# Batch 0 of a fused attention and two FFNs: both heads in one product, zeros beside keys and values, and two weight pieces made earlier

## Chip, cores and metric

One core of one Trainium2 chip. The metric is the device time of one execution in microseconds (us). The kernel before takes 851.62 us, the median of 3 runs (851.27 to 851.75).

## What is computed

Attention with a window mask (4 batches, 8 heads, 576 positions, head size 64), and then two FFNs over the 2304 tokens, all in float32:

```python
scores = scale * np.matmul(q, k.transpose(0, 1, 3, 2))
mask_plain = (rel >= 0) & (rel < 32)                          # heads 0 to 3
mask_dil = (rel >= 0) & (rel < 128) & (rel % 4 == 0)          # heads 4 to 7
attn = softmax(np.where(mask, scores, -1e9))                  # sum + 1e-9
x = (attn @ v) as (2304, 512)
h = x @ w_in                                                  # FFN 1, d_ff 2048
x = (np.maximum(h, 0) + alpha * np.minimum(h, 0)) @ w_out
h = x @ w_in2                                                 # FFN 2
out = np.where(h >= 1, h, np.where(h <= -1, 0, (h + 1) ** 2 / 4)) @ w_out2
```

## The kernel before

**Attention in groups.** The host reorders the positions of the dilated heads, so that each block of 32 queries needs 64 neighbouring keys. A batch then has 6 groups (NGB), and the 4 batches 24 (NG). A group holds 3 x 4 blocks (n, j) of 32 queries, for two heads at once; the upper 64 partitions hold the second head's data. Each group goes through the same steps: scores (TensorE, the mask is added by a product with the identity), maximum and subtraction (VectorE), exp (ScalarE), turn (TensorE transposes, ScalarE copies the result to pT), values (TensorE), norm (VectorE: sum, reciprocal, product) and out (TensorE transposes, ScalarE copies into XA, the input of FFN 1).

**Batch 0 has its own form** (`e_scores` L166, `e_exp` L184, `e_values` L195). One tile `e_in` per group, six in all, holds keys, queries and values; each group is loaded by two DMAs over all 128 partitions (L119, L127) from the array `a0`. The two heads are separate products of 64 rows, 12 blocks x 2 heads for scores (L180) and as many for values (L204); float32 products count twice in the profile, so 48 each. Scores and values have one PSUM tile each, of two banks (tags s2 and o2).

**Batches 1 to 3** use `a_scores` L133 and `a_values` L216: one product of 128 rows for both heads. For that, `qk` (two buffers) holds keys of head 0 with zeros beside them for head 1, and the reverse in the upper half; `vz` (two buffers) does so for the values. The loads L122, L123 and L131 fill 64 partitions each, the last in runs of 4 x 65 floats. The zeros are written once, by memsets on GpSimd (L745 to L749 and, for the whole of qk0, L803).

**Weights.** A weight piece (128 x 1024 words, 512 KB) is loaded by `w_load` L265 into one of five staging tiles and made into float32 by three VectorE steps (`w_make` L308: L320, L321, L314). `conv(k)` issues the next k such steps; `more()` loads further pieces while staging tiles are free. A made piece of w_in is split into a high and a low part by ScalarE (L326) and GpSimd or VectorE (L327), in `w_split`; the input XA is split the same way in `x_split` L423.

**The order is written out by hand** (`tc.manual_schedule()`): every engine, and the DMA queue of SyncE (SP), works through its instructions in program order. At the start SP issues the loads of all six groups of batch 0, with one weight piece behind group 0 and one behind group 2 (FIRST), and TensorE runs 10 warm-up products. The loop at L786 then runs the six groups, each a step behind the next (scores of group i, turn of i-1, out of i-2, values of i-1), and at i = 0 and 2 makes a weight piece. At i = 3, after the first x_split and the memset of qk0, SP gets the loads of group 6 (the first of batch 1) and the next pieces. Behind the loop (L810 to L833) stand the last steps of groups 4 and 5, four conv steps and the first hidden products of FFN 1 (`f_h` L503, for two f, in quarters by input chunk c; L513, L514 and L515 are its three products), each behind the x_split of its chunk.

Then come the slots (`slot` L898), one per f: hidden product f, activation, output product of the f before (`f_y`, L688 to L690), one attention step of a later batch, and conv steps. The constants EARLY (5, 6) say how many conv steps slots 0 and 1 issue; from slot 2 on it is 6.

Of the kernel before, what the change touches and what calls it, by code (L numbers as in the profile page):

```python
# [22 lines left out]
P = 128  # L23
# [35 lines left out]

EARLY = (5, 6)  # L60
READY = 12
# [20 lines left out]
def _key_offset(g, m):  # L82

    return SUB * m + (WIN if g % 3 == 1 and m >= 6 else 0)


@with_exitstack
def attention_then_two_ffns(ctx: ExitStack, tc: tile.TileContext, a0, aqk, av, w1i, w1o, w2i, w2o, alpha, masks, ident, out):
    nc = tc.nc
# [19 lines left out]
    vzt = [wp.tile([P, VZ], F32, tag=f"vz{i}", name=f"vz{i}") for i in range(2)]  # L109
    vz = [t[:, :GS * 2 * 4 * DS].rearrange("p (n h j d) -> p n h j d", n=GS, h=2, j=4) for t in vzt]  # L110

# [3 lines left out]


    def a_load_qk(i):
        if i < NGB:
            nc.sync.dma_start(e_in[i][:, :QK], a0[i, :, :QK])  # L119
        elif i < NG:  # L120
            t = qk[i % 2]
            nc.sync.dma_start(t[:D, :QK], aqk[i - NGB, :D])  # L122
            nc.sync.dma_start(t[D:, KW:], aqk[i - NGB, D:])  # L123

    def a_load_v(i):
        if i < NGB:
            nc.sync.dma_start(e_in[i][:, QK:], a0[i, :, QK:])  # L127
        elif i < NG:
            for h in range(2):
                r = slice(h * D, (h + 1) * D)  # L130
                nc.sync.dma_start(vz[i % 2][r, :, h].rearrange("p n j d -> p n (j d)"), av[i - NGB, r])  # L131

    def a_scores(i, pool, tag, add_on_pe):  # L133
        ps = pool.tile([P, GS, 2, KEYS], F32, tag=tag, name="s_ps")
        sb0 = (i % NGB) * GS
        t = qk[i % 2]
        mk = mask[:, sb0:sb0 + GS, None, :].to_broadcast([P, GS, 2, KEYS])
# [27 lines left out]

    def e_scores(i):  # L166

        ps = ps_e.tile([P, 2, TW], F32, tag="s2", name="s_ps")
        t = e_in[i]
        mk = mask[:, i * GS:(i + 1) * GS]  # L170
        for h in range(2):
            nc.tensor.matmul(ps[:, h, :GS * KEYS].rearrange("p (n k) -> p n k", n=GS), idb, mk, start=True, stop=False)
        for n in range(GS):
            for j in range(4):
                r = slice(j * SUB, (j + 1) * SUB)
                k0 = _key_offset(i, 4 * n + j)
                for h in range(2):
                    p = slice(h * D, (h + 1) * D)
                    q = t[p, KW + n * P + j * SUB:KW + n * P + (j + 1) * SUB]
                    nc.tensor.matmul(ps[r, h, n * KEYS:(n + 1) * KEYS], q, t[p, k0:k0 + KEYS], start=False, stop=n == GS - 1)  # L180
        sc_t[i] = ps

    def e_exp(i):
        ps = sc_t.pop(i)  # L184
        s = buf(i, "s").rearrange("p (n k) -> p n k", k=KEYS)
        src = ps[:, :, :GS * KEYS].rearrange("p h (n k) -> p h n k", n=GS)
        mx = st_p.tile([P, 2 * GS], F32, tag="mx", name="mx")
        mx = mx.rearrange("p (h n) -> p h n", h=2)
        nc.vector.tensor_reduce(mx, src, AX.X, ALU.max)
        nc.vector.tensor_tensor(  # L190
            s.rearrange("p (n h) k -> p h n k", h=2), src, mx[:, :, :, None].to_broadcast([P, 2, GS, KEYS]), ALU.subtract)
        nc.scalar.activation(s, s, AF.Exp, scale=SCALE)
        s_t[i] = s

    def e_values(i):  # L195
        pT = pT_t.pop(i)
        ps = ps_e.tile([P, 2, TW], F32, tag="o2", name="o_ps")
        v = e_in[i][:, QK:].rearrange("p (n j d) -> p n j d", n=GS, j=4)
        for n in range(GS):
            for j in range(4):  # L200
                r = slice(j * SUB, (j + 1) * SUB)
                for h in range(2):
                    p = slice(h * D, (h + 1) * D)
                    nc.tensor.matmul(ps[r, h, n * DS:(n + 1) * DS], pT[p, n, r], v[p, n, j], start=True, stop=True)  # L204
        a_norm(i, ps[:, :, :GS * DS].rearrange("p h (n d) -> p n h d", n=GS))

    def a_turn(i, pool, tag):
# [8 lines left out]
    def a_values(i, pool, tag):  # L216
        pT = pT_t.pop(i)
        ps = pool.tile([P, GS, 2, DS], F32, tag=tag, name="o_ps")
        for n in range(GS):
            for j in range(4):  # L220
                r = slice(j * SUB, (j + 1) * SUB)
                nc.tensor.matmul(ps[r, n], pT[:, n, r], vz[i % 2][:, n, :, j], start=True, stop=True)  # L222
        a_norm(i, ps)
# [488 lines left out]
    with tc.manual_schedule(), ExitStack() as late:  # L712
        first = ExitStack()
        sp = first.enter_context(tc.tile_pool(name="sp", bufs=1))
        ps_e = first.enter_context(tc.tile_pool(name="ps_e", bufs=1, space=bass.MemoryType.PSUM))
        e_in = [sp.tile([P, QK + GS * 4 * DS], F32, name=f"e_in{i}") for i in range(NGB)]

# [16 lines left out]

        for i in range(NGB):
            a_load_qk(i)
            a_load_v(i)
            if i in FIRST:
                w_load(*pend_l.pop(0))
            if i == 1:  # L740
                nc.sync.dma_start(mask[:, 2 * GS:], masks[:, 2 * GS:])
        nc.sync.dma_start(al, alpha)
        nc.scalar.activation(half, half, AF.Exp, scale=0.0)
        nc.scalar.activation(half, half, AF.Copy, scale=0.5)
        nc.gpsimd.memset(qk[1][:D, QK:], 0.0)  # L745
        nc.gpsimd.memset(qk[1][D:, :KW], 0.0)
        for i in range(2):
            nc.gpsimd.memset(vz[i][:D, :, 1], 0.0)
            nc.gpsimd.memset(vz[i][D:, :, 0], 0.0)  # L749

# [13 lines left out]
        def more():  # L764

            while not hold and pend_l and st_free:
                w_load(*pend_l.pop(0))
# [18 lines left out]
        for i in range(NGB):  # L786
            e_scores(i)
            if i >= 1:
                a_turn(i - 1, ps_a, "a")
            e_exp(i)  # L790
            if i >= 2:
                a_out(i - 2, ps_a, "w")
            else:
                fill(2)
            if i >= 1:
                e_values(i - 1)
            w_cut()
            if i in FIRST:
                conv(3)
            if i == 3:  # L800
                x_split(n0, 0, True)

                nc.gpsimd.memset(qk[0], 0.0)  # L803
                hold = False
                a_load_qk(NGB)
                w_load(*pend_l.pop(0))
                w_load(*pend_l.pop(0))
                a_load_v(NGB)
                more()
            if i == 4:  # L810
                x_split(n0, 1, True)
        w_cut()
# [4 lines left out]
        conv(1)  # L817
        e_values(NGB - 1)
        x_split(n0, 2)
# [314 lines left out]
def _attention_layout(q, k, v):  # L1134
# [67 lines left out]
```

## Time and profile before

| What | us |
|---|---|
| median of 3 runs | 851.62 |
| lowest and highest run | 851.27 and 851.75 |
| the profiled execution | 853.01 |
| its span, first to last instruction | 851.2 |
| TensorE busy in the span | 835.7 |
| VectorE busy | 556.0 |
| GpSimd busy | 483.4 |
| ScalarE busy | 428.6 |

The profile is of one execution. PE is TensorE, PEld its weight loads (which lie beside its products), DVE is VectorE, ACT ScalarE, POOL GpSimd, SP SyncE, which issues the DMAs. A name such as L514 is a line of the kernel. Times in views are counted from the first instruction. "DMA share" is the mean busy share of the core's 16 DMA engines, and "PEclk" the clock that TensorE was granted, as a share of 2.4 GHz.

### The profile page before, as it was taken

What the parts mean: (1) busy time and instruction counts of PE and PEld (TensorE: products, weight loads), DVE (VectorE), ACT (ScalarE), POOL (GpSimd) and SP (SyncE); (2) the same over time, 40 slices, a digit from 0 to 9 for tenths busy, and PEclk for the clock granted to TensorE, in tenths of its full rate; (3) what the DMA queues carried; (4) which work ended last, traced back from release to release, by engine and by line L of the source; (5) the groups of instructions that cost most, each with busy time, mean ns of one, the idle gap of its engine ahead of it and who ended that gap; (6) DMA issues with size and microseconds to landing.
All of it is one profiled execution on the core that took longest, in us unless ns stands there. A gap on an engine that the chain in (4) does not pass through costs nothing.

```text
span 851.2 us, 14291 instructions
## 1 busy us (share of the span) xinstructions
PE 835.7 (98%) x5330; PEld 687.2 (81%) x5330; DVE 556.0 (65%) x911; ACT 428.6 (50%) x803; POOL 483.4 (57%) x411
## 2 busy tenths in 40 slices
PE   6999999999999999999999999999999999999998
PEld 3667778998777878888888888888888888888898
DVE  4798787666775676766688776776428677640243
ACT  3444444665435565555444565564435555443364
POOL 2465656777434677667348666763652423346486
PEclk9899999999999999999999999999999999999999
DMA  8798665864630025354287745243836553547210
GB/s 301 226 259 233 200 170 178 262 192 132 199 118 25 1 83 202 112 163 159 99 334 292 264 157 209 105 181 123 314 128 218 192 181 126 171 152 293 77 74 25
DMA packets 54980, 147.45 MB, mean 173 GB/s; under 512 B 5632, under 2 KB 13440, under 8 KB 54912
## 3 DMA queue, kind: packets, MB, share of 16 engines
q1 hardware_dynamic: 54624, 146.39, 51.1%
q8 instruction: 42, 0.69, 0.3%
q14 instruction: 26, 0.21, 0.1%
q10 hardware_dynamic: 288, 0.16, 0.1%
HBM read 101.97 MB, written 44.56 MB: 172 GB/s over the span
## 4 chain that ended last, share of the span: by engine, by line
PE 81%; DVE 7%; DMA 5%; ACT 3%; issue 2%; POOL 1%; SPq 0%; ACTq 0%; DVEq 0%; POOLq 0%
PE y L688 14%; PE y L690 14%; PE y L689 14%; PE h_ps L544 7%; PE h_ps L545 7%; PE h_ps L546 7%; PE h_ps L513 5%; PE h_ps L515 4%; PE h_ps L514 4%; DMA gd<-XA 3%; PE o_ps L222 2%; PE s_ps L148 1%; ACT wr L326 1%; PE t_ps L211 1%; DVE w_ps L320 1%
## 5 line engine op out<-in xcount | busy, mean ns | idle before, releaser
L327 POOL TENSOR_TENSOR wol<-wo,woh 128x512 fp32r<-128x512 f32 x153 | 201.2, 1322 | 76.6 <-ACT woh L326 76.2
L688 PE MATMUL y<-gh,wol 128*128 128x512 f32 (+1 forms) x444 | 164.0, 369 | 0.6 <-POOL wol L327 0.6
L690 PE MATMUL y<-gl,woh 128*128 128x512 f32 (+1 forms) x444 | 160.2, 361 | 0.0
L689 PE MATMUL y<-gh,woh 128*128 128x512 f32 (+1 forms) x444 | 160.1, 361 | 0.0
L327 POOL TENSOR_TENSOR wr<-wb,wr 128x512 fp32r<-128x512 f32 x60 | 77.8, 1297 | 124.6 <-ACT wr L326 123.7
L327 POOL TENSOR_TENSOR wr<-wi,wr 128x512 fp32r<-128x512 f32 x50 | 64.6, 1293 | 124.3 <-ACT wr L326 123.0
L544 PE MATMUL h_ps<-xv,wr 128*128 128x512 f32 x336 | 130.8, 389 | 0.2 <-DVE wf L314 0.2
L545 PE MATMUL h_ps<-xv,wr 128*128 128x512 f32 x336 | 130.8, 389 | 0.0
L546 PE MATMUL h_ps<-xv,wr 128*128 128x512 f32 x336 | 130.8, 389 | 0.0
L326 ACT ACTIVATE woh<-wo 128x512 fp32r<-128x512 f32 x153 | 93.6, 626 | 67.6 <-PE y L690 51.0
L688 PEld LDWEIGHTS y<-gh,wol 128*128 128x128 f32 x444 | 83.7, 189 | 16.6 <-POOL wol L327 2.3
L690 PEld LDWEIGHTS y<-gl,woh 128*128 128x128 f32 x444 | 83.6, 188 | 13.3
L689 PEld LDWEIGHTS y<-gh,woh 128*128 128x128 f32 x444 | 83.8, 189 | 12.2
L513 PE MATMUL h_ps<-xv,wr 128*128 128x512 f32 (+1 forms) x256 | 90.2, 352 | 0.4
L514 PE MATMUL h_ps<-xv,wr 128*128 128x512 f32 (+1 forms) x256 | 86.2, 337 | 0.2 <-DVE xv L327 0.2
L515 PE MATMUL h_ps<-xv,wr 128*128 128x512 f32 (+1 forms) x256 | 86.4, 337 | 0.0
L558 ACT ACTIVATE g<-g,half 128x512 f32<-128x512 f32 x64 | 44.8, 723 | 72.2 <-DVE g L557 71.0
L689 PE MATMUL y<-gx,woh 128*128 128x512 f32 x192 | 75.4, 392 | 0.0
L690 PE MATMUL y<-gx,woh 128*128 128x512 f32 x192 | 75.3, 392 | 0.0
L688 PE MATMUL y<-gx,wol 128*128 128x512 f32 x192 | 75.3, 392 | 0.0
L544 PEld LDWEIGHTS h_ps<-xv,wr 128*128 128x128 f32 x336 | 63.1, 188 | 13.8 <-issue 0.6
L545 PEld LDWEIGHTS h_ps<-xv,wr 128*128 128x128 f32 x336 | 63.1, 188 | 13.2
(122 smaller groups left out, 1515.1 us busy)
## 6 DMA issues: line engine op xcount, KB each, us to landing
gd<-XA SPq DMA_DIRECT2D x42, 512.0 KB, 3.4
gx<-gd SPq DMA_DIRECT2D x42, 512.0 KB, 6.5
wb<-whole SPq DMA_DIRECT2D x30, 512.0 KB, 4.6
st<-w1i SPq DMA_DIRECT2D x16, 512.0 KB, 6.0
st<-w1o SPq DMA_DIRECT2D x16, 512.0 KB, 6.0
st<-w2i SPq DMA_DIRECT2D x16, 512.0 KB, 4.6
st<-w2o SPq DMA_DIRECT2D x16, 512.0 KB, 4.7
kept<-wr SPq DMA_DIRECT2D x16, 512.0 KB, 2.7
```

What stands on the lines that cost most here:

```text
L326: nc.scalar.activation(hi, src, AF.Copy)
L327: low_on.tensor_tensor(lo, src, hi.bitcast(F32), ALU.subtract)
L513: nc.tensor.matmul(ps[:, :w], r[:, 1, cs], x[:, 0, xs], start=(c == 0), stop=False)
L514: nc.tensor.matmul(ps[:, :w], r[:, 0, cs], x[:, 1, xs], start=False, stop=False)
L515: nc.tensor.matmul(ps[:, :w], r[:, 0, cs], x[:, 0, xs], start=False, stop=(c == NC - 1))
L544: nc.tensor.matmul(o, w[:, 1, cs], x[:, 0], start=start and m == 0, stop=False, skip_group_check=not start)
L545: nc.tensor.matmul(o, w[:, 0, cs], x[:, 1], start=False, stop=False, skip_group_check=not start)
L546: nc.tensor.matmul(o, w[:, 0, cs], x[:, 0], start=False, stop=m == 1, skip_group_check=not start)
L558: nc.scalar.activation(t, t, AF.Square, bias=half, scale=0.5)
L688: nc.tensor.matmul(o, wl[:, cs], gh[:, :w], start=(i == 0), stop=False)
L689: nc.tensor.matmul(o, wh[:, cs], gh[:, :w], start=False, stop=False)
L690: nc.tensor.matmul(o, wh[:, cs], gl[:, :w], start=False, stop=(i == NF - 1))
```

## The change

Batch 0 takes the form of the other batches: `e_scores`, `e_exp`, `e_values` and `a0` go, and the loop calls `a_scores`, `a_less`, `a_exp` and `a_values` with PSUM tiles of one bank that alternate (s0/s1 and o0/o1). There are four buffers of qk and of vz for batch 0, two of them in place of the e_in tiles. All get their zeros at the start: qk from VectorE, vz from GpSimd. Groups 0 to 3 are loaded at the start; 4 and 5 when the buffers of groups 0 and 1 are free again, and behind them two more weight pieces. Those are made (conv(3)) at i = 4 and i = 5; x_split 0 and 1 stay at i = 3 and 4, now behind this conv. The loads of group 6 move to i = 4 and 5. EARLY falls from (5, 6) to (2, 3).

```diff
-EARLY = (5, 6)
+EARLY = (2, 3)
...
+    def at_buf(i):
+        return i if i < 4 else i % 2
+
     def a_load_qk(i):
-        if i < NGB:
-            nc.sync.dma_start(e_in[i][:, :QK], a0[i, :, :QK])
-        elif i < NG:
-            t = qk[i % 2]
-            nc.sync.dma_start(t[:D, :QK], aqk[i - NGB, :D])
-            nc.sync.dma_start(t[D:, KW:], aqk[i - NGB, D:])
+        if i < NG:
+            t = qk[at_buf(i)]
+            nc.sync.dma_start(t[:D, :QK], aqk[i, :D])
+            nc.sync.dma_start(t[D:, KW:], aqk[i, D:])
 
     def a_load_v(i):
-        if i < NGB:
-            nc.sync.dma_start(e_in[i][:, QK:], a0[i, :, QK:])
-        elif i < NG:
+        if i < NG:
             for h in range(2):
                 r = slice(h * D, (h + 1) * D)
-                nc.sync.dma_start(vz[i % 2][r, :, h].rearrange("p n j d -> p n (j d)"), av[i - NGB, r])
+                nc.sync.dma_start(vz[at_buf(i)][r, :, h].rearrange("p n j d -> p n (j d)"), av[i, r])
...
-        e_in = [sp.tile([P, QK + GS * 4 * DS], F32, name=f"e_in{i}") for i in range(NGB)]
+        qk += [sp.tile([P, QK + KW], F32, name=f"qk{i}") for i in (2, 3)]
+        vz += [vz_view(sp.tile([P, VZ], F32, name=f"vz{i}")) for i in (2, 3)]
...
-        for i in range(NGB):
+        for i in range(4):
+            nc.vector.memset(qk[i][:D, QK:], 0.0)
+            nc.vector.memset(qk[i][D:, :KW], 0.0)
+            nc.gpsimd.memset(vz[i][:D, :, 1], 0.0)
+            nc.gpsimd.memset(vz[i][D:, :, 0], 0.0)
+        for i in range(4):
             a_load_qk(i)
             a_load_v(i)
             if i in FIRST:
...
-        nc.gpsimd.memset(qk[1][:D, QK:], 0.0)
-        nc.gpsimd.memset(qk[1][D:, :KW], 0.0)
-        for i in range(2):
-            nc.gpsimd.memset(vz[i][:D, :, 1], 0.0)
-            nc.gpsimd.memset(vz[i][D:, :, 0], 0.0)
...
         for i in range(NGB):
-            e_scores(i)
+            a_scores(i, ps_e, f"s{i % 2}", True)
+            if i < 2:
+                a_load_qk(i + 4)
+            if i == 4:
+                hold = False
+                a_load_qk(NGB)
+                more()
             if i >= 1:
                 a_turn(i - 1, ps_a, "a")
-            e_exp(i)
+            a_less(i)
+            a_exp(i)
             if i >= 2:
                 a_out(i - 2, ps_a, "w")
             else:
                 fill(2)
             if i >= 1:
-                e_values(i - 1)
+                a_values(i - 1, ps_e, f"o{i % 2}")
+                if i < 3:
+                    a_load_v(i + 3)
+                    if i == 2:
+                        w_load(*pend_l.pop(0))
+                        w_load(*pend_l.pop(0))
+                elif i == 5:
+                    a_load_v(NGB)
             w_cut()
-            if i in FIRST:
+            if i in FIRST or i >= 4:
                 conv(3)
-            if i == 3:
-                x_split(n0, 0, True)
-
-                nc.gpsimd.memset(qk[0], 0.0)
-                hold = False
-                a_load_qk(NGB)
-                w_load(*pend_l.pop(0))
-                w_load(*pend_l.pop(0))
-                a_load_v(NGB)
-                more()
-            if i == 4:
-                x_split(n0, 1, True)
+            if i in (3, 4):
+                x_split(n0, i - 3, True)
         w_cut()
         f_h(n0, 0, (0,))
         f_h(n0, 1, (0,))
...
-        e_values(NGB - 1)
+        a_values(NGB - 1, ps_e, "o0")
```

The host prepares `aqk` and `av` for all four batches, with no `a0`.

## Rows read from the trace of the kernel before

**Rows 1.** Windows: start:end, length, then busy us (instructions) of PE, PEld, DVE, ACT, POOL, then PEclk, DMA share, GB/s.

```profile
36.10:58.00 21.90, 19.84 (x152) 14.43 (x153) 21.17 (x35) 10.11 (x19) 12.85 (x10) 1.00 1.05 283
20.60:27.40 6.80, 6.19 (x182) 4.57 (x183) 3.38 (x9) 3.48 (x7) 4.54 (x4) 0.50 0.16 43
60.00:70.00 10.00, 10.00 (x90) 7.58 (x89) 8.57 (x16) 4.00 (x8) 4.84 (x5) 1.00 0.85 243
```

**Rows 2.** Chain of waits, 35 to 58 us: start, length, who.

```profile
35.32 0.69 DVE xv L327
...
57.88 0.55 PE t_ps L211 x3
```

**Rows 3.** Timeline, TensorE in batch 0: start, length, what [idle before, releaser].

```profile
14.94 0.72 PE L204 MATMUL o_ps<-e_in,pT 64*32 64x65 f32 x48 [1.80 <-ACT XA L255]
...
21.21 0.66 PE L204 MATMUL o_ps<-e_in,pT 64*32 64x65 f32 x25 [3.08 <-issue]
```

**Rows 4.** Timeline, first work of VectorE and GpSimd on data, and L514.

```profile
7.29 0.56 DVE L189 TENSOR_REDUCE mx<-s_ps 128x6 f32<-128x384 f32 x1 [6.15 <-PE s_ps L180]
...
12.50 1.27 POOL L327 TENSOR_TENSOR wr<-wi,wr 128x512 fp32r<-128x512 f32 x1 [7.67 <-ACT wr L326]
...
36.07 0.50 PE L514 MATMUL h_ps<-xv,wr 128*128 128x512 f32 x1 [0.23 <-DVE xv L327]
```

**Rows 5.** Chain of waits: scores in both forms, values in the new form.

```profile
11.68 0.67 PE s_ps L180 x45
...
61.19 0.80 PE o_ps L222 x24
...
65.22 0.65 PE s_ps L148 x24
```

**Rows 6.** Groups by line, 0 to 37 us: count, busy us, mean ns, idle before.

```profile
L190 DVE TENSOR_TENSOR s<-s_ps,mx 128x384 f32<-128x384 f32 x6 | 3.3, 558 | 0.5
...
L314 DVE SCALAR_TENSOR_TENSOR wi<-st,wi 128x512 int32<-128x512 int32 x3 | 2.1, 693 | 0.1
...
L749 POOL MEMSET vz<- 64x780 f32 x2 | 1.5, 743 | 0.1
L327 DVE TENSOR_TENSOR xv<-XA,xv 128x512 fp32r<-128x512 f32 x2 | 1.4, 687 | 0.2 <-ACT xv L326 0.2
...
L320 DVE TENSOR_SCALAR wi<-st 128x512 int32<-128x512 int32 x3 | 1.3, 420 | 1.1 <-DMA st<-w1i 1.1
...
L229 DVE RECIPROCAL rs<-rs 128x6 f32<-128x6 f32 x6 | 1.1, 191 | 0.2
```

**Rows 7.** Timeline of SP, the two loads of vz of group 6.

```profile
27.89 1.23 SPq L131 DMA_DIRECT2D vz<-av  x2
```

**Rows 8.** DMA issues, 0 to 60 us: count, KB each, median us to landing.

```profile
st<-w1i SPq DMA_DIRECT2D x9, 512.0 KB, 8.6
...
qk<-aqk SPq DMA_DIRECT2D x8, 208.0 KB, 9.6
vz<-av SPq DMA_DIRECT2D x6, 195.0 KB, 10.2
mask<-masks SPq DMA_DIRECT2D x1, 192.0 KB, 6.4
```

**Rows 9.** Windows with 64-partition loads, and one (the last) of weight pieces alone.

```profile
63.50:65.50 2.00, 2.00 (x31) 1.45 (x33) 1.90 (x4) 1.07 (x2) 1.78 (x2) 1.00 1.04 236
...
27.00:28.00 1.00, 0.98 (x6) 0.74 (x6) 0.90 (x2) 0.31 (x1) 0.75 (x1) 0.80 0.97 300
31.00:32.50 1.50, 1.25 (x52) 0.91 (x51) 0.67 (x3) 1.36 (x4) 0.00 (x0) 1.00 0.93 275
39.00:42.00 3.00, 2.52 (x13) 1.75 (x11) 2.92 (x6) 1.28 (x4) 2.85 (x2) 1.00 1.08 227
...
35.00:38.50 3.50, 3.19 (x37) 1.80 (x35) 3.19 (x6) 1.48 (x4) 1.29 (x1) 1.00 1.02 405
```

**Rows 10.** DMA issues, 24.9 to 25.1 us: one half of qk on an idle queue.

```profile
qk<-aqk SPq DMA_DIRECT2D x1, 208.0 KB, 3.9
```

More of the change, by code (lines that the diff above doesn't have):

```diff
@@ L87, in attention_then_two_ffns @@
 @with_exitstack
-def attention_then_two_ffns(ctx: ExitStack, tc: tile.TileContext, a0, aqk, av, w1i, w1o, w2i, w2o, alpha, masks, ident, out):
+def attention_then_two_ffns(ctx: ExitStack, tc: tile.TileContext, aqk, av, w1i, w1o, w2i, w2o, alpha, masks, ident, out):
     nc = tc.nc
@@ L109, in attention_then_two_ffns, with vz_view @@
     vzt = [wp.tile([P, VZ], F32, tag=f"vz{i}", name=f"vz{i}") for i in range(2)]
-    vz = [t[:, :GS * 2 * 4 * DS].rearrange("p (n h j d) -> p n h j d", n=GS, h=2, j=4) for t in vzt]
+    def vz_view(t):
+        return t[:, :GS * 2 * 4 * DS].rearrange("p (n h j d) -> p n h j d", n=GS, h=2, j=4)
+    vz = [vz_view(t) for t in vzt]
     sc_t, s_t, pT_t, o_t = {}, {}, {}, {}
+    def at_buf(i):
+        return i if i < 4 else i % 2
     def a_load_qk(i):
-        if i < NGB:
-            nc.sync.dma_start(e_in[i][:, :QK], a0[i, :, :QK])
-        elif i < NG:
-            t = qk[i % 2]
-            nc.sync.dma_start(t[:D, :QK], aqk[i - NGB, :D])
-            nc.sync.dma_start(t[D:, KW:], aqk[i - NGB, D:])
+        if i < NG:
+            t = qk[at_buf(i)]
+            nc.sync.dma_start(t[:D, :QK], aqk[i, :D])
+            nc.sync.dma_start(t[D:, KW:], aqk[i, D:])
     def a_load_v(i):
-        if i < NGB:
-            nc.sync.dma_start(e_in[i][:, QK:], a0[i, :, QK:])
-        elif i < NG:
+        if i < NG:
             for h in range(2):
                 r = slice(h * D, (h + 1) * D)
-                nc.sync.dma_start(vz[i % 2][r, :, h].rearrange("p n j d -> p n (j d)"), av[i - NGB, r])
+                nc.sync.dma_start(vz[at_buf(i)][r, :, h].rearrange("p n j d -> p n (j d)"), av[i, r])
     def a_scores(i, pool, tag, add_on_pe):
@@ L135, in a_scores @@
         sb0 = (i % NGB) * GS
-        t = qk[i % 2]
+        t = qk[at_buf(i)]
         mk = mask[:, sb0:sb0 + GS, None, :].to_broadcast([P, GS, 2, KEYS])
@@ L164, in a_exp @@
         nc.scalar.activation(s_t[i], s_t[i], AF.Exp, scale=SCALE)
[L166 to L205, printed above, removed]
     def a_turn(i, pool, tag):
@@ L221, in a_values @@
                 r = slice(j * SUB, (j + 1) * SUB)
-                nc.tensor.matmul(ps[r, n], pT[:, n, r], vz[i % 2][:, n, :, j], start=True, stop=True)
+                nc.tensor.matmul(ps[r, n], pT[:, n, r], vz[at_buf(i)][:, n, :, j], start=True, stop=True)
         a_norm(i, ps)
@@ L1159, in _attention_layout @@
     aq, ak, av = groups(aq), ak.reshape(NG, P, KW), groups(av)
-    a0 = np.concatenate([ak[:NGB], aq[:NGB], av[:NGB]], axis=2)
-    aq, ak, av = aq[NGB:], ak[NGB:], av[NGB:]
     lower = np.concatenate([ak[:, :D], aq[:, :D]], axis=2)
     upper = np.concatenate([aq[:, D:], ak[:, D:]], axis=2)
-    return a0, np.concatenate([lower, upper], axis=1), np.ascontiguousarray(av).reshape(NG - NGB, P, GS, 4 * DS)
+    return np.concatenate([lower, upper], axis=1), np.ascontiguousarray(av).reshape(NG, P, GS, 4 * DS)
 def _w_in(w):
@@ L1181 @@
     nc = bacc.Bacc("TRN2", target_bir_lowering=False, num_devices=1, dynamic_dma_scratch_size=1024)
-    a0, aqk, av = _attention_layout(q, k, v)
+    aqk, av = _attention_layout(q, k, v)
     arrays = {
-        "a0": a0,
         "aqk": aqk,
```

## The prediction

> **What bounds the kernel now.** I read the windows first, for where TensorE waits; then the chain of waits over the first 60 us; then the timeline of that stretch; last the DMA views, because the change touches the input loads. TensorE is full from 60 us on: 10.00 us busy of 10.00 [rows 1]. Work in that part can't be shortened by a change to batch 0, so the time can move only by what TensorE loses before it. From 36.1 to 58.0 it is busy 19.84 of 21.90 us, so 2.06 us are lost [rows 1]. The chain says to whom: from 35.32 us it runs on VectorE, weight piece after weight piece, and passes to TensorE only at 57.88 [rows 2]. Before 36 us the losses are larger: the value products waited 1.80 us at 14.94 and 3.08 us at 21.21 (the latter for nothing that the profile shows) [rows 3], and a stretch of 6.8 us from 20.6 on ran at a granted clock of 0.50, the 1.2 GHz level [rows 1]. One marker stands for all of it: the first hidden product's last quarter, L514, starts at 36.07, released by VectorE's x_split [rows 4]. If it starts later, the end is later, less what is regained behind it.
>
> **The change part by part.** *Products.* 48 score matmuls of 64 rows become 24 of 128 rows with zeros; both forms are in the trace: 0.67 us for a group in the old form, 0.65 in the new [rows 5]; values 0.72 [rows 3] against 0.80 [rows 5]. I cost this at nothing: TensorE waits for inputs in this stage anyway. If that cover went, it would be 6 x 0.06 = 0.4 us. Alternating PSUM buffers let scores(i+1) start before VectorE has emptied scores(i); worth nothing while the next keys are late.
>
> *Zeros.* GpSimd gets 8 memsets of vz instead of 4, at 0.74 us [rows 6]: 6.2 us from 0.7 us on, done by 7; its first work is at 12.50 [rows 4]. VectorE gets 8 memsets of 64x448, smaller than those, so at most 0.74 us each: done by 7.1 us, and its first use is at 7.29 [rows 4]. Both are hidden, just. The whole-tile memset of qk0 before group 6 goes; only the start of late loads waited for it. The zeroed and the loaded ranges are disjoint. Should the loads wait for memsets all the same, the first would go out after two of VectorE's, about 1.3 us later, and all others with it: bounds 0 and 1.3 us, I take 0.
>
> *SP.* A group takes four issues instead of two; the two for vz alone hold SP for 1.23 us [rows 7], those for qk about as long, some 2.4 us a group. That is under what the transfers of a group take (next), so it is hidden; on an emptier queue it would be 2.4 us a group.
>
> *Loads.* This term decides. Bytes are the same, 2 x 208 + 2 x 195 KB a group [rows 8], but each transfer now fills 64 partitions, and v in short runs, where batch 0 so far had 128-partition rows. In the trace of before only batches 1 to 3 are loaded so. The 512 KB weight pieces, with 128 partitions, alone move at 405 GB/s; in windows that hold the 64-partition loads the queue gives 300, 275, 227 and 236 GB/s at a DMA share of 0.93 to 1.08 [rows 9], so the engines are full and slower. I take the mean of these four, 260 GB/s; the ends for the range are 227 and 300.
>
> Where such a rate bites is the new **wait**: the third piece (w2) is loaded behind v(5) and made by VectorE after norm(3), in the middle of group 4. VectorE works in order, so while w2 is in flight the maxima of group 5 stand behind it, then exp, turn, values, norm and output of group 5, x_split(2) and (3), and L514. When does w2 land? The first keys land about 5.2 us (second half issued near 1.25, 3.9 us to landing [rows 10]). Behind them come v(0) 0.40 MB, five groups of 0.825, three pieces of 0.524 and the masks' 0.20: 6.3 MB. At 260 GB/s that is 24.2 us: **w2 lands at 29.4 us** (26.2 at 300, 33.0 at 227). Without it VectorE would be through norm(3) some microseconds earlier, as the keys of group 5 are 1.3 MB (5 us) ahead of w2.
>
> From the landing VectorE has one unbroken row of work before L514 [rows 6]: making w2 0.42 + 0.69 + 0.69, with gaps 1.85; maximum and subtraction of group 5 1.2; norm(4) 0.95; making w3 1.85 (it lands 2.0 us behind w2, so no wait); first step of w4 0.43; norm(5) 0.95; x_split(2) 0.69; two steps of w4 1.4; x_split(3) 0.69. The sum is 10.0 us. ScalarE and TensorE deliver between these (exp, turn and values of group 5 take some 2.5 us while norm(4) and w3 are made). So L514 starts at 39.4 to 39.5 instead of 36.07: **+3.4 us**.
>
> *Fewer steps in the first two slots.* Slots 0 and 1 lose 3 steps each, 6 x 0.69 = 4.1 us of VectorE [rows 6], in the stretch that VectorE bounded. TensorE can regain at most its 2.06 us [rows 1]. The first group of batch 1 still takes its way through VectorE and ScalarE, so I take 1.4, with ends 0 and 2.06: **-1.4 us**. Behind slot 1 the pieces are as far as before.
>
> *Clock.* Before, 3.08 us without a matmul came shortly ahead of the 0.50 stretch. Now TensorE has little to do from about 28 us (values(4) and the first quarter of the hidden products are done) until group 5's turn at w2 + 3.6 = 33 us. A second such stretch near 34 to 41 us would lie partly on the saturated part. 6.8 us at half speed cost at most 3.4 us, and nothing where TensorE waits anyhow; I take **+2.0 us**, ends 0 and 3.4.
>
> **Sum:** 3.4 - 1.4 + 2.0 = +4.0 us. The profiled execution took 853.01 us (span 851.2), so it would become 857.0; it lay 1.39 us above the median of the runs, 851.62, and the median is forecast at 855.6 us.
>
> The Trainium skill has a rule that speaks against this change: "SBUF — State Buffer", section "Door 1: The DMA port swizzle", says that a transfer to 64 partitions reaches only 8 of the 16 ports, 196 GB/s measured, and the section "Can I just issue two DMAs to hit both halves?" that two such transfers don't add up. The trace agrees in direction, 227 GB/s against 405, but its first window, 300 GB/s with qk halves in it, is well above the page's figure [rows 9]. By 196 GB/s w2 would land, as an estimate, at 37 us, and the sum would be about +12 us.
>
> **The rivals.** *(B) Faster: the loads are fast in this stage.* In the opening nothing else loads the queue, and TensorE's old stalls are gone. Weights at 405 GB/s and the other 4.7 MB at 300 make 19.6 us: w2 lands at 24.8, L514 starts at 34.8, -1.2; all 2.06 us are regained, and no clock stretch: -3.3, **848.3 us**. For it: the 300 GB/s window is the one with an otherwise empty queue. Against it: the new opening fills the queue from the first microsecond. It decides if w2 lands before about 26 us.
>
> *(C) The port limit holds throughout: 227 GB/s.* Then w2 lands at 33.0, L514 starts at 43.0, +7.0 - 1.4 + 2.0 = +7.6, **859.2 us**. For it: the 227 and 236 windows are the ones in a saturated queue, as here. Against it: they also hold weight pieces that were slowed, and the halves of two transfers can overlap. The sections of the Trainium skill's page "SBUF — State Buffer" named above would give this case its reason.
>
> *(D) The change does not do what it says:* the third and fourth piece come no earlier than needed, and what slots 0 and 1 save is spent in front of L514. At 275 GB/s w2 lands at 28.1, L514 starts at 38.1, +2.1, all 2.06 us regained, no clock stretch: **851.6 us**.
>
> **How the numbers follow.** My forecast, w2 landing between about 28.5 and 32 with some loss by the clock, 0.42; C 0.22; D 0.19; B 0.17. A measurement of this kernel can tell about 0.2%, 1.7 us, from no change. B and the lower edge of D are faster by more: 0.19. The rest of D is the same: 0.17. The forecast and C are slower: 0.64. The range takes the ends of the rate: from 849.4, leaving out the better half of B, to 860.2, which holds C with up to 1 us from the memsets or the clock. That leaves out about 0.2. The likeliest case alone spans 853.5 to 858.
>
> **What would show it.** Right: the L320 of the third weight piece idles some microseconds for a DMA of st, group 5's maximum follows only after it, L514 starts near 39.5 us; the windows from 5 to 25 us show some 260 GB/s at a full DMA share; TensorE's loss between L514 and 58 us is under 1 us; a granted clock of 0.50 shows near 34 to 41 us. Wrong: 350 GB/s or more in the opening, or a w2 that has landed when VectorE comes to it (then B or D); VectorE's row of work in front of L514 broken by waits for another engine (then the 10.0 us are too short); TensorE still waiting 2 us after L514, which would say that the pieces were not its bound; a loss behind 60 us, where I forecast none.

## The result: 857.6 us, slower by 0.64%

The change takes **857.62 us**, the median of 6 runs (five of 856.19 to 857.79, whose median is 857.48, and one disturbed execution of 1188.85 us at a mean clock of 0.654, which the ratio leaves out). The kernel before took 851.68 us beside it (6 runs, 851.25 to 852.61). The ratio is **1.0064, 95% interval 1.005 to 1.0078**. The forecast was 855.6 us, range 849.4 to 860.2, slower at 0.64.

The profiled execution of after took 856.19 us (span 854.4). It was the shortest of its runs, while the profiled one of before, 853.01, lay above its median. So the two traces differ by 3.2 us of span, the medians by 5.9; what may fill that difference comes with the clock, below. In this text L476 of after is L514 of before, L282, L283 and L276 are the steps of a weight piece (L320, L321, L314), L289 is L327, L288 is L326, L158 the maximum, L190 the start of the norm, L151 the scores, L173 the turn and L184 the values of all groups.

The windows of after, columns as in [rows 1]:

```profile
5.00:10.00 5.00, 2.97 (x36) 1.37 (x34) 2.64 (x6) 0.52 (x1) 1.90 (x3) 1.00 1.05 279
10.00:15.00 5.00, 4.00 (x61) 2.73 (x66) 2.13 (x6) 1.42 (x3) 0.36 (x1) 0.66 1.10 244
...
20.00:25.00 5.00, 2.97 (x78) 2.25 (x71) 2.56 (x6) 2.66 (x6) 1.36 (x2) 1.00 1.07 234
...
30.00:35.00 5.00, 2.44 (x14) 1.82 (x11) 4.14 (x10) 1.37 (x3) 0.00 (x0) 0.91 1.04 318
35.00:40.00 5.00, 5.00 (x41) 3.76 (x40) 4.86 (x9) 2.26 (x7) 1.54 (x1) 0.75 1.06 320
41.30:60.00 18.70, 18.35 (x147) 13.78 (x148) 17.46 (x29) 9.57 (x18) 11.91 (x9) 1.00 0.99 255
60.00:70.00 10.00, 10.00 (x89) 7.59 (x89) 7.65 (x14) 3.69 (x7) 6.44 (x6) 1.00 0.66 195
```

The DMA engines are full (share 1.04 to 1.10 in the first five rows), yet move 234 to 244 GB/s in the windows from 10 and 20 us, which hold halves of batch 0 and little else. TensorE is busy 2.97 of 5 us in 20 to 25 and 2.44 of 5 in 30 to 35. Behind L476 it now loses 0.35 us (18.35 of 18.70) where [rows 1] lost 2.06, and from 60 us on it is full as before.

The timeline of after, columns as in [rows 3]: VectorE from the third piece to L476, then TensorE's long waits and L476 itself:

```profile
30.59 0.43 DVE L282 TENSOR_SCALAR wi<-st 128x512 int32<-128x512 int32 x1 [2.24 <-DMA st<-w1i]
...
32.39 0.55 DVE L158 TENSOR_REDUCE mx<-s_ps 128x6 f32<-128x384 f32 x1
...
35.58 1.65 DVE L276 SCALAR_TENSOR_TENSOR wo<-st,wo 128x512 int32<-128x512 int32 x1
...
10.70 1.51 PE L151 MATMUL s_ps<-qk 128*32 128x128 f32 x24 [2.73 <-DMA qk<-aqk]
...
19.74 0.86 PE L151 MATMUL s_ps<-qk 128*32 128x128 f32 x24 [1.86 <-DMA qk<-aqk]
...
24.47 0.86 PE L151 MATMUL s_ps<-qk 128*32 128x128 f32 x24 [1.67 <-DMA qk<-aqk]
...
34.21 0.90 PE L173 MATMUL t_ps<-idt,s 128*128 128x128 f32 x3 [2.56 <-ACT s L167]
41.26 0.50 PE L476 MATMUL h_ps<-xv,wr 128*128 128x512 f32 x1 [0.23 <-DVE xv L289]
```

VectorE stands 2.24 us for the third piece (w2); group 5's maximum, whose scores were done at 28.1, follows only at 32.39; TensorE stands 2.56 us for group 5's turn; and L476 starts at 41.26 against 36.07 [rows 4], +5.19. The old stalls of the value products [rows 3] are gone, but TensorE stands for keys instead: 2.73, 1.86 and 1.67 us in front of the scores of groups 1, 3 and 4.

The chain of waits of after, columns as in [rows 2], and the work of GpSimd that lies beside L276 (timeline):

```profile
23.73 6.84 DMA st<-w1i
...
39.84 0.64 ACT xv L288
...
40.51 0.69 DVE xv L289
```

```profile
35.13 1.54 POOL L289 TENSOR_TENSOR wr<-wi,wr 128x512 fp32r<-128x512 f32 x1 [5.22 <-ACT wr L288]
```

So w2 lands at 30.57. Between the turn at 34.21 and x_split(3) at 40.51 this chain runs over TensorE and ScalarE; VectorE's own row beside it ends at 40.38, only 0.1 us sooner.

### The profile page after: what moved, and what is told of

Its sections match the earlier page's. It is cut to its first block, busy times and chain, and to the rows that moved or that the text cites. A ratio compares the mean times of both kernels' runs of the same rounds, so it can differ in the third digit from the quotient of the medians.

```text
span 854.4 us, 13767 instructions
## 1 busy us (share of the span) xinstructions
PE 836.9 (98%) x5053; PEld 688.4 (81%) x5054; DVE 559.8 (66%) x919; ACT 428.9 (50%) x803; POOL 484.4 (57%) x412
## 4 chain that ended last, share of the span: by engine, by line
PE 92%; DMA 2%; DVE 2%; ACT 1%; POOL 1%; SPq 1%; issue 1%; DVEq 0%; ACTq 0%
PE y L650 16%; PE y L652 15%; PE y L651 15%; PE h_ps L506 9%; PE h_ps L507 9%; PE h_ps L508 9%; PE h_ps L475 5%; PE h_ps L477 5%; PE h_ps L476 5%; PE o_ps L184 2%; PE s_ps L151 2%; PE x_ps L199 1%; DMA qk<-aqk 1%; PE t_ps L173 1%; DMA st<-w1i 1%; DMA vz<-av 1%
## 5 line engine op out<-in xcount | busy, mean ns | idle before, releaser
L289 POOL TENSOR_TENSOR wol<-wo,woh 128x512 fp32r<-128x512 f32 x153 | 200.9, 1320 | 77.7 <-ACT woh L288 77.3
L289 POOL TENSOR_TENSOR wr<-wb,wr 128x512 fp32r<-128x512 f32 x60 | 77.7, 1295 | 125.1 <-ACT wr L288 124.3
L289 POOL TENSOR_TENSOR wr<-wi,wr 128x512 fp32r<-128x512 f32 x50 | 65.1, 1302 | 123.4 <-ACT wr L288 122.4
L288 ACT ACTIVATE woh<-wo 128x512 fp32r<-128x512 f32 x153 | 93.5, 626 | 67.6 <-PE y L652 51.0
L476 PE MATMUL h_ps<-xv,wr 128*128 128x512 f32 (+1 forms) x256 | 86.2, 337 | 0.2 <-DVE xv L289 0.2
```

The lines of the kernel that those rows point to most:

```text
L288: nc.scalar.activation(hi, src, AF.Copy)
L289: low_on.tensor_tensor(lo, src, hi.bitcast(F32), ALU.subtract)
L476: nc.tensor.matmul(ps[:, :w], r[:, 0, cs], x[:, 1, xs], start=False, stop=False)
```

## The experiments

Two marks are read from the timeline of every run: the product that stands for L514 (36.07 us before), and the start of the scores of group 9, their product with the mask (64.88 before), behind which the order is the old one. Their difference is what slots 0 and 1 give back. The second mark in before (L141) and in after (L144):

```profile
64.88 0.35 PE L141 MATMUL s_ps<-mask,idt 128*32 128x384 bf16 x4
...
67.89 0.35 PE L144 MATMUL s_ps<-mask,idt 128*32 128x384 bf16 x4
```

| run | median us | ratio, 95% | profiled, us | L514 | group 9 |
|---|---|---|---|---|---|
| the change | 857.62 | 1.0064 [1.005, 1.0078] | 856.19 | +5.19 | +3.01 |
| pieces_alone | 852.16 | 1.0006 [0.9997, 1.0016] | 851.81 | +1.59 | -0.60 |
| products_alone | 856.64 | 1.0054 [1.0041, 1.0066] | 856.64 | +3.55 | +3.54 |
| halves | 857.54 | 1.0065 [1.0051, 1.0078] | 857.64 | +4.93 | +4.90 |
| runs | 852.22 | 1.0005 [0.9996, 1.0014] | 852.90 | -0.91 | -0.94 |
| wait_moved | 856.12 | 1.005 [1.0036, 1.0064] | 855.26 | +4.38 | +2.19 |
| pieces_late | 851.31 | 0.9997 [0.9988, 1.0005] | 852.33 | +2.08 | -0.17 |
| queues | 856.92 | one run | 856.92 | +4.14 | +4.13 |
| count | 852.92 | one run | 852.92 | +0.45 | +0.40 |
| fills | 857.54 | 1.0064 [1.0052, 1.0076] | 858.62 | +6.98 | +4.81 |
| wide | 855.14 | 1.0038 [1.0026, 1.005] | 856.21 | +5.82 | +3.65 |
| wide_alone | 853.16 | 1.002 [1.0011, 1.0029] | 852.53 | +0.02 | -0.02 |
| wide_moved | 855.61 | 1.0041 [1.0029, 1.0053] | 854.05 | +3.43 | +1.24 |

### The two parts apart: pieces_alone and products_alone

The kernel before, with only the two early pieces:

```diff
-EARLY = (5, 6)
+EARLY = (2, 3)
...
+            if i == 2:
+                w_load(*pend_l.pop(0))
+                w_load(*pend_l.pop(0))
             w_cut()
-            if i in FIRST:
+            if i in FIRST or i >= 4:
                 conv(3)
...
-                w_load(*pend_l.pop(0))
-                w_load(*pend_l.pop(0))
```

> The kernel before with the second half of the change alone: two pieces loaded at i = 2, behind batch 0's inputs, and made at i = 4 and 5, EARLY (2, 3); products and loads of batch 0 as before. Theory (64-partition loads are what makes the change slower): the pieces land by about 23 us, VectorE does not wait for them, L514 starts 0.7 to 1.5 us later than in the kernel before, and some 2 us are regained behind it: 850.7 us, between 849.5 and 851.5. Rival (the pieces themselves are the loss, their making stands in front of group 5): L514 3 us later or more, 853 to 855 us.

Its time is no different from before's, a miss for the 850.7 us that were expected. In the trace the mark of L514 is 1.59 us late, since two pieces now stand in front of it, and 2.2 us come back in the slots; the 0.60 us that are left don't show in the median. Here the loads are over early (the windows of pieces_alone):

```profile
15.00:20.00 5.00, 3.52 (x92) 2.39 (x79) 3.66 (x8) 1.36 (x4) 0.00 (x0) 0.55 1.04 396
20.00:25.00 5.00, 4.26 (x129) 3.15 (x129) 2.03 (x5) 2.70 (x7) 3.61 (x3) 0.50 0.23 90
```

The change without the early pieces:

```diff
-EARLY = (2, 3)
+EARLY = (5, 6)
...
-                    if i == 2:
-                        w_load(*pend_l.pop(0))
-                        w_load(*pend_l.pop(0))
...
-            if i in FIRST or i >= 4:
+            if i in FIRST:
                 conv(3)
```

> The changed kernel without the two early pieces: no loads at i = 2, no conv at i = 4 and 5, EARLY (5, 6). Theory (the slow loads act through the third piece, behind which group 5's maximum stands): the maximum of group 5 starts near 28.4 instead of 32.4 us, the first hidden product's last quarter near 37.3 us, and the wait behind it is as in the kernel before: about 853 us, between 852 and 855. Rival (slow inputs alone carry the loss): that quarter starts near 41 us and the time stays at 857 us or above. Rival (products with zeros cost nothing and the inputs are hidden): 851.7 us.

The loss is nearly whole, with no wait for w2 in front of group 5's maximum. The timeline of products_alone:

```profile
29.91 0.55 DVE L158 TENSOR_REDUCE mx<-s_ps 128x6 f32<-128x384 f32 x1
...
39.62 0.51 PE L476 MATMUL h_ps<-xv,wr 128*128 128x512 f32 x1 [0.22 <-DVE xv L289]
```

Group 5's maximum starts at 29.91, 2.5 us sooner than in the change, and still 3.5 us are lost at L476. VectorE does wait for the third piece here too, whose load now goes out later: 2.64 us, but behind norm(4) (timeline). The chain of waits in front of L476 shows that this wait is not what ends last:

```profile
35.38 0.43 DVE L282 TENSOR_SCALAR wi<-st 128x512 int32<-128x512 int32 x1 [2.64 <-DMA st<-w1i]
```

```profile
18.58 7.39 DMA qk<-aqk
...
38.20 0.65 ACT xv L288
...
38.87 0.69 DVE xv L289
```

It runs from the landing of a group's keys over the steps of groups 4 and 5 to x_split(3), with no weight piece in it. So late inputs are enough, and the wait for w2 alone is not the cause. A miss for the 853 us that the expectation took.

### What in the loads: halves, runs, queues

The kernel before with each load of batch 0 cut at partition 64, rows as long as they were (halves; the keys and queries likewise), or with v in runs of 1040 bytes over all 128 partitions (runs):

```diff
...
-            nc.sync.dma_start(e_in[i][:, QK:], a0[i, :, QK:])
+            nc.sync.dma_start(e_in[i][:D, QK:], a0[i, :D, QK:])
+            nc.sync.dma_start(e_in[i][D:, QK:], a0[i, D:, QK:])
```

```diff
+    VR = 4 * DS + 4
...
-            nc.sync.dma_start(e_in[i][:, QK:], a0[i, :, QK:])
+            nc.sync.dma_start(e_v(i), a0[i, :, QK:].rearrange("p (n x) -> p n x", n=GS))
...
```

> The kernel before with each input load of batch 0 cut into two of 64 partitions, rows as long as before; nothing else. Theory (64 partitions are what slows the loads): 5 to 20 us at 250 to 290 GB/s instead of 400, the last values land 4 to 6 us later, and the time is 1 to 3 us above the kernel before, about 853.5 us. Rival (the short runs of v are what slows them): 380 GB/s or more, 851.7 us.

> The kernel before with the values of batch 0 loaded in runs of 1040 bytes over all 128 partitions (a gap of 16 bytes between runs in the tile); nothing else. Theory (64 partitions are what slows the loads): v costs some 0.4 us more per group, 330 GB/s or more from 5 to 18 us, the time within 1 us of the kernel before. Rival (the short runs are what slows them): 250 to 280 GB/s and 1 to 3 us more, about 853.5 us.

Cutting the loads brings the whole loss by itself, 1.0065, with before's products and order of pieces; short runs bring none. The windows of halves:

```profile
5.00:10.00 5.00, 2.26 (x56) 1.13 (x55) 2.12 (x4) 0.52 (x1) 0.00 (x0) 1.00 1.04 277
10.00:15.00 5.00, 4.28 (x110) 2.42 (x110) 2.66 (x7) 1.42 (x3) 1.02 (x1) 0.66 1.05 244
...
20.00:25.00 5.00, 3.65 (x78) 2.45 (x77) 3.51 (x7) 1.60 (x5) 0.00 (x0) 0.50 1.05 253
18.00:31.00 13.00, 10.63 (x302) 7.34 (x305) 6.61 (x16) 5.14 (x11) 4.10 (x4) 0.50 0.76 179
```

The windows of runs:

```profile
5.00:10.00 5.00, 3.91 (x109) 2.07 (x107) 3.12 (x6) 0.97 (x2) 0.00 (x0) 1.00 1.05 397
10.00:15.00 5.00, 2.77 (x135) 2.23 (x137) 2.77 (x7) 2.80 (x6) 1.26 (x1) 1.00 1.06 383
```

At the same full DMA share, windows of loads to 64 partitions show 244 to 277 GB/s and windows of loads to 128 some 390. In halves the loads are also twice as many and half as large, and no run takes that apart from the 64 partitions; time lost between transfers it is not, since the engines are as busy as in runs (share 1.04 to 1.06).

The expectation had the rate about right and the time 4 us too low. Two things stand beside the rate. The granted clock is 0.50 for 13 us, from 18 to 31, where before had 6.8 [rows 1]; what that costs here no run shows. And the chain of waits of halves does run over the third piece:

```profile
30.30 6.72 DMA st<-w1i
...
37.04 0.43 DVE wi L322
```

Its load goes out behind those of group 6, which wait for the memset of qk0 on GpSimd (28.01 to 29.13), itself late with the groups. So halves shows what cutting the loads costs in all, not by which way.

In queues, the upper halves of groups 0 and 1 go out from ScalarE's queue:

```diff
...
-            nc.sync.dma_start(e_in[i][D:, QK:], a0[i, D:, QK:])
+            (nc.scalar if i < 2 else nc.sync).dma_start(e_in[i][D:, QK:], a0[i, D:, QK:])
```

> The run with halves again, with the upper halves of groups 0 and 1 issued from ScalarE's queue instead of SP's. Theory (a half reaches only part of the paths into the memory, and halves of opposite kind can use both): the values of group 1 land near 10.5 us instead of 12.4, at 330 GB/s or more from 4 to 9 us. Rival (two transfers of halves share the same engines and do not add up): 12 us or later, 240 to 290 GB/s.

The windows of queues:

```profile
5.00:10.00 5.00, 2.15 (x53) 1.11 (x52) 0.76 (x2) 1.69 (x3) 0.00 (x0) 0.83 1.02 261
10.00:15.00 5.00, 3.55 (x68) 1.96 (x76) 3.19 (x6) 1.41 (x4) 0.00 (x0) 0.50 1.06 232
```

They show 232 to 261 GB/s, as the rival said: a lower and an upper half under way from two queues don't add up. That agrees with the Trainium skill, "SBUF — State Buffer", section "Can I just issue two DMAs to hit both halves?".

### The wait for the third piece: wait_moved and pieces_late

The change, with w2 made behind group 5's subtraction; and the kernel before with both pieces loaded at step 2 but only one made early, at step 5 (EARLY (4, 4)). The diff is that of wait_moved:

```diff
             a_less(i)
+            if i == 5:
+                conv(3)
...
-            if i in FIRST or i >= 4:
+            if i in FIRST or i == 5:
                 conv(3)
```

> The changed kernel with the making of its third piece moved from the end of group 4's steps to behind group 5's subtraction. Theory after the first runs (the inputs in halves carry the loss, VectorE's wait for the third piece adds about 1 us of it): group 5's maximum starts near 28.4 instead of 32.4 us, the last quarter of the first hidden product about 1.2 us earlier, 856.4 us, between 855.6 and 857.0. Rival (the wait for the third piece is the carrier): 853 to 854 us. Rival (it costs nothing): 857.6 us.

> The kernel before with the two pieces loaded at i = 2, but one of them made at i = 5 and nothing at i = 4, EARLY (4, 4), so three steps less in slots 0 and 1 instead of six. Theory (in pieces_alone the making at i = 4 stands in front of group 5 and gives back what the slots gain): L514 within 0.5 us of the kernel before, 1 to 1.5 us regained behind it, 850.5 us, between 849.8 and 851.3. Rival (the gain is lost elsewhere, in the wait of the value products or the clock): 851.7 to 852.5 us.

The timeline of wait_moved:

```profile
28.53 0.55 DVE L158 TENSOR_REDUCE mx<-s_ps 128x6 f32<-128x384 f32 x1
...
30.95 0.43 DVE L282 TENSOR_SCALAR wi<-st 128x512 int32<-128x512 int32 x1 [1.22 <-DMA st<-w1i]
...
40.45 0.50 PE L476 MATMUL h_ps<-xv,wr 128*128 128x512 f32 x1 [0.22 <-DVE xv L289]
```

Group 5's maximum comes 3.9 us sooner (28.53 for 32.39), but L476 only 0.8 us (40.45 for 41.26), and the median 1.5 us, about as expected. The rest of VectorE's row still stands behind the landing, and the inputs are as late.

pieces_late shows no gain and no loss. Its mark of L514 is 2.08 us late, where at most 0.5 was expected. The timeline of pieces_late:

```profile
37.40 0.69 DVE L327 TENSOR_TENSOR xv<-XA,xv 128x512 fp32r<-128x512 f32 x1 [1.60 <-ACT xv L326]
```

No piece is waited for here: TensorE's products in front of it ran at a granted clock of 0.51 (33.4 to 36.5 us), and x_split(3) stands 1.60 us behind them.

### The clock: fills

The change, with four warm-up products more in steps 2 to 5:

```diff
             if i >= 2:
                 a_out(i - 2, ps_a, "w")
+                fill(4)
             else:
                 fill(2)
```

> The changed kernel with four small products of zeros (about 1.1 us of TensorE) added in each of the loop's steps 2 to 5, where TensorE else waits. Theory (the clock term is part of the loss): the stretch of granted clock 0.50 near 34 us goes or moves ahead of 30 us, where TensorE waits for inputs anyway, L477 stays near 41.3 us, and the time falls by 1 to 2 us, to about 856.0. Rival (the clock costs nothing here, since the stretch lies where TensorE waits): 857.6 as the change. If the fillers delay the groups instead: 858 to 859, with L477 later than 41.8.

(The product behind x_split(3) is L476 in this kernel too.) The windows of fills:

```profile
30.00:35.00 5.00, 4.95 (x90) 3.60 (x80) 3.27 (x8) 1.79 (x3) 1.27 (x1) 1.00 1.04 278
35.00:40.00 5.00, 3.97 (x39) 2.40 (x37) 4.79 (x11) 2.76 (x7) 1.56 (x1) 1.00 1.02 351
```

The timeline of fills:

```profile
32.47 0.49 DVE L282 TENSOR_SCALAR wi<-st 128x512 int32<-128x512 int32 x1 [0.83 <-DMA st<-w1i]
...
43.05 0.50 PE L476 MATMUL h_ps<-xv,wr 128*128 128x512 f32 x1 [0.23 <-DVE xv L289]
```

The stretch at half clock near 34 us is gone (1.00 where the change has 0.91 and 0.75). From the third piece to L476 pass 10.58 us, in the change 10.67: there the half clock cost 0.1 us, since VectorE's row stands beside it (its end at 40.38 against 40.48 of ScalarE, above). The piece came 1.9 us later in this execution, and the median did not move: the rival was right. The mean clock of the six runs did not rise either (0.994 to 0.996, in the change 0.993 to 0.995), so this run doesn't price the clock in the others.

### Inputs over 128 partitions in the new form: wide, wide_alone, wide_moved

The change, with the queries of both heads in one transfer and v in one transfer into a staging tile, from which GpSimd copies each half between the zeros. Only the keys still go in halves. The values of groups 4 and 5 are now loaded with their keys, since the staging tiles are free sooner:

```diff
+            nc.sync.dma_start(t[:D, :KW], aqk[i, :D, QK - KW:])
+            nc.sync.dma_start(t[D:, QK:], aqk[i, D:, QK - KW:])
+            nc.sync.dma_start(t[:, KW:QK], aqk[i, :, :QK - KW])
...
+    def a_spread_v(i):
+        for h in range(2):
+            r = slice(h * D, (h + 1) * D)
+            nc.gpsimd.tensor_copy(vz[at_buf(i)][r, :, h].rearrange("p n j d -> p n (j d)"), vs[i % 4][r])
...
+            nc.sync.dma_start(vs[i % 4], av[i])
...
```

> The changed kernel with batch 0's inputs loaded over 128 partitions where that can be: queries of both heads in one transfer, values in one transfer into a staging tile, from which GpSimd copies each head's half between the zeros; only the keys still go in halves. Per group 0.59 MB at 400 GB/s and 0.23 MB at 250: 2.4 us instead of 3.3. Theory (late inputs carry the whole loss, products and early pieces cost nothing): the third piece lands near 23 us and VectorE no longer waits for it, the first L476 behind group 5 starts at 36 us or before, and of the pieces 1.4 to 2.2 us stay: 849.5 to 850.5. Rival 1 (the early pieces give nothing to the end, as in the kernel of before with them): 851.5 to 852.2. Rival 2 (the new order of the steps carries a loss of its own): 855 or more with early inputs. Rival 3: GpSimd's twelve copies of some 0.8 us hold up the splits of the weights, and L476 starts 2 us later: 853 to 854.

The inputs came in time (group 5's scores at 25.18, before 25.52), but the third piece did not: its load went out at 21.90 and took 7.6 us to land, where 23 us were expected. The time missed what was expected by 4.6 us or more. The timeline of wide (L292 and L168 are L282 and L158 there):

```profile
29.50 0.55 DVE L292 TENSOR_SCALAR wi<-st 128x512 int32<-128x512 int32 x1 [3.07 <-DMA st<-w1i]
31.93 0.55 DVE L168 TENSOR_REDUCE mx<-s_ps 128x6 f32<-128x384 f32 x1
...
41.14 0.69 DVE L299 TENSOR_TENSOR xv<-XA,xv 128x512 fp32r<-128x512 f32 x1 [1.22 <-ACT xv L298]
...
41.89 0.50 PE L486 MATMUL h_ps<-xv,wr 128*128 128x512 f32 x1 [0.23 <-DVE xv L299]
```

Of the 5.82 us at the mark 1.22 are not VectorE's row: x_split(3) (L299) stands for ScalarE, behind products at a granted clock of 0.50 (33.7 to 39.1 us). The rest stands behind the wait for the third piece. The time is also the one of rival 2 (the new order of steps carries a loss of its own); wide_alone, next, speaks against it.

So the last two runs each take another part away: wide_alone makes no early piece, wide_moved makes w2 behind the subtraction (the edit of wait_moved).

```diff
-EARLY = (2, 3)
+EARLY = (5, 6)
...
-            if i in FIRST or i >= 4:
+            if i in FIRST:
                 conv(3)
```

> The kernel with the wide loads and GpSimd's copies (the run named wide), but the two early pieces are not made in batch 0 (EARLY (5, 6), conv(3) at steps 0 and 2 alone); they are still loaded at step 2. Theory (two latenesses stand beside each other, the inputs' and the third piece's, and either alone carries the whole loss): with the inputs on time and no piece in front of group 5's maximum, that maximum starts at 26 to 27.5 us, the quarter behind x_split(3) (L476 of the page of after, L486 here) at 35 to 37 us, and the time is 851.0 to 852.5, no change against before. Rival 1 (the products in one piece or the new order of steps carry a loss of their own): 854 or more with that maximum on time. Rival 2 (with half the instructions and without TensorE's waits there is a gain): 850.0 or less.

> The run named wide with the third piece made behind group 5's subtraction, not ahead of its maximum. There VectorE waited 3.07 us for the piece, which landed at 29.48, with the inputs on time. Theory (the two latenesses stand beside each other): with both taken away group 5's maximum starts at 26 to 27.5 us, the rest of VectorE's row (norm(4), the fourth piece and on) still stands behind the landing, so L486 starts at 38 to 39.5 us, 2 to 3 us earlier than in wide, and of that 2.2 us are regained in the first two slots: 851.5 to 853. Rival (the pieces' landing sets the end whatever stands in front of it): 854.5 to 855.5 as wide.

The timeline of wide_alone:

```profile
26.34 0.55 DVE L168 TENSOR_REDUCE mx<-s_ps 128x6 f32<-128x384 f32 x1
...
36.09 0.50 PE L486 MATMUL h_ps<-xv,wr 128*128 128x512 f32 x1 [0.23 <-DVE xv L299]
```

The timeline of wide_moved:

```profile
26.52 0.55 DVE L168 TENSOR_REDUCE mx<-s_ps 128x6 f32<-128x384 f32 x1
...
28.65 1.02 DVE L292 TENSOR_SCALAR wi<-st 128x512 int32<-128x512 int32 x1 [0.92 <-DMA st<-w1i]
...
39.50 0.50 PE L486 MATMUL h_ps<-xv,wr 128*128 128x512 f32 x1 [0.22 <-DVE xv L299]
```

With both latenesses gone L486 starts at 36.09, where L514 stood before (36.07), and the trace is level from there on (-0.02 at group 9). The median is 0.2% above before all the same, 853.16, a little over what was expected; its runs fall in two sets, 852.1 to 853.3 at a mean clock of 0.997 or 0.998 (7 runs), and 854.3 to 856.1 at 0.994 or 0.996 (5 runs). In wide_moved the trace gains what was expected (+1.24 at group 9, profiled 854.05), the median, 855.61, is the rival's; its clock was 0.993 in three of six runs.

### TensorE's old stalls: count

The kernel before with 27 products more ahead of the groups, 32 small ones in place of five of the warm-up:

```diff
-        fill(WARM)
+        fill(WARM - 5)
+        for _ in range(32):
+            nc.tensor.matmul(warm_ps[:, :64], warm[:, :P], warm[:, :64], start=True, stop=True)
```

> The kernel before with 5 of the 10 warm-up products replaced by 32 small ones, so that every later TensorE instruction has 54 more ahead of it. Theory (the 1.80 and 3.08 us in the value products are waits for TensorE's own instructions, which come in blocks): both waits move about 54 instructions up the program: the first out of the start of values(1) into scores(2), the second out of the middle of values(2) to the end of scores(3) or the transposes behind it. Rival (waits for data or another engine): both stay at the same product.

The timeline of count, TensorE:

```profile
12.22 0.44 PE L180 MATMUL s_ps<-e_in 64*32 64x64 f32 x28
13.41 0.41 PE L180 MATMUL s_ps<-e_in 64*32 64x64 f32 x20 [0.74 <-issue]
...
19.77 0.52 PE L237 MATMUL x_ps<-idt,o 128*128 128x128 f32 x3 [2.75 <-DVE s L190]
```

Both stalls of [rows 3] moved ahead by some 27 products: the first from the front of values(1) to 20 products before the end of scores(2), with a turn and an out (6 products) between; the second from behind 23 products of values(2) to the front of the out ahead of them. They hang on how many instructions TensorE has run, not on data. The change, with half as many in batch 0, shows neither, and gains nothing by it, because it stands for keys.

## Why the prediction was right, and where its steps were not

**The rate** held. 260 GB/s from the first keys on were forecast; w2 landed at 30.57, and 6.3 MB in the 25.0 us from the first keys (5.5) make 252 GB/s; the four windows from 5 to 25 us have a mean of 259 (that from 15, not shown above, has 278). It was forecast at 29.4: 0.4 us by the first keys, 0.8 by the rate. The rule of the Trainium skill, "SBUF — State Buffer", section "Door 1: The DMA port swizzle", gave the direction, and halves shows the cut at partition 64 to cost the rate; by its 196 GB/s the landing would have been at 37 us, as an estimate. That estimate takes the weight pieces, which fill 128 partitions, at 196 too; with them at the 405 of [rows 9] it is some 33 us. The windows show 232 to 279 in stages of halves, so the sum by rows was nearer.

**The wait** is there as forecast (L282, 2.24 us, then the maximum). But the sentence that without it VectorE would be through norm(3) some microseconds earlier, and so the wait carries the loss, **failed**: it counted one lateness where two stand beside each other. Late inputs alone carry +3.54 to group 9 (products_alone, with no piece in its chain); the early pieces with their wait, and 1.2 us of half clock, carry +3.65 (wide); both together +3.01, and cutting the old kernel's loads +4.90 (halves). With both away there is nothing left (wide_alone, -0.02). Taking one away (wait_moved, wide) shows the other.

**VectorE's row** was forecast at 10.0 us and is 10.7 (30.59 to 41.26): L276 took 1.65 us at 35.58 instead of 0.69. It began while GpSimd split a weight part (L289, 35.13 to 36.67), and so did other lengthened steps: L320 of before, 1.53 us at 35.93, beside L327 at 35.89; L286 of wide, 1.64 us at 35.13, beside L299 at 34.73. That one makes the other wait is argued, not tested. Nor is the row quite unbroken: x_split(3) waits 0.1 us for ScalarE at its end. With the landing 1.2 us later the row gives +5.19 for the +3.4 of the forecast: the term was too small by 1.8.

**Slots 0 and 1** give back 2.2 us, not 1.4. So do all seven runs with fewer steps there whose two marks stand in the table (2.2 to 2.3), the change's own included, and the others none; pieces_alone, pieces_late, wait_moved, fills, wide and wide_moved differ in everything in front of L514. The upper end, 2.06 of [rows 1], was nearer than the value taken: between the two marks TensorE's idle time falls from 2.06 to 0.35 us, and the time that the profile counts as busy for the same products by another 0.47. Three steps fewer (pieces_late) give back as much as six.

**The clock**, +2.0 us, is not in the profiled execution: the stretch at 0.50 (34.1 to 37.5) was there, shorter than forecast, and lay beside VectorE's row, where it costs 0.1 us (fills). So the trace's own sum is +5.19 - 2.18 = +3.01 at group 9, below the +4.0 forecast. It came that near in part by luck: the terms were off by +1.8, -0.8 and -2.0. A stretch at half clock is not always free: x_split(3) stood 1.22 us behind one in wide and 1.60 in pieces_late. Over the runs the new form seems to pay for the clock as well: the change's two end runs are 856.19 at 0.995 and 857.79 at 0.993, wide_alone's two sets lie some 2 us apart, whereas 20 runs of before at 0.998 had a middle of 851.3, 8 at 0.994 one of 852.1 and 13 at 0.993 one of 851.8. Where the stretches lie in the runs without a profile is not known, so that this is the whole of the 2.7 us between +3.2 by the traces and +5.9 by the medians is argued, not shown.

**Costed at nothing, and right:** the products (wide_alone, L486 at 36.09), the memsets (first scores at 5.58, before 5.96) and SP's issues (the queue is full throughout).

**The rivals.** B and D needed w2 by 26 or 28 us; even the runs with seven tenths of the inputs' bytes in wide transfers landed it at 29.5 (wide) and 28.6 (wide_moved). C (227 GB/s, 859.2 us) missed the median by 1.6 us, hardly less than the forecast's 2.0, but not for its reason: w2 landed 2.4 us before C's 33.0, and L476 came at 41.26, not 43.0.

## What to carry to other kernels

Before cutting a load at a partition boundary to make room for zeros, work out when its last byte lands at the rate that the trace shows for such transfers; a layout that saves products can cost more in the queue than the engine ever had to give. Where a step is late by two causes beside each other, taking one away shows little, so take both away before a part is called harmless or guilty, and read from the chain of waits which of them ends last. What a later stage can take back is read from the idle time of the bound engine there, and it comes back whole only if the work in front of that stage does not grow by more.

## What the runs showed of the hardware

- Windows of loads to 64 partitions show 232 to 279 GB/s at a full DMA share, in runs of 1040 bytes (the change) or long rows (halves), from one queue or two (queues); loads of the same bytes to 128 partitions 383 to 397, even in runs of 1040 bytes (runs).
- TensorE stood 1.80 and 3.08 us at places fixed by the number of its own instructions (count), the first with the DMA queue full, the second while it ran empty (share 0.19 from 18 to 21 us); the profile names no releaser or a wrong one. That these are waits for its instructions fits packets of an instruction queue ahead of them in the trace, and is argued.
- Executions of one kernel differ in their mean clock by up to 0.006 (pieces_late, 0.992 to 0.998). A stretch at half clock costs 0.1 us where VectorE's row stands beside it (fills), and 1.2 to 1.6 us where x_split(3) stands behind TensorE's products (wide, pieces_late). A difference of 0.2% between two kernels wants several runs of each, and a single trace can stand some 1.5 us from its median on either side.
